# First attention chunk: its steps re-ordered, probabilities and the next keys' split moved behind the last head, scores two heads ahead, one weight load on GpSimd's queue

## The chip, the cores and the metric

One core of a Trainium2 chip runs the whole program. The metric is the time of one execution on the device in microseconds. The kernel is written with a tile framework: the program lists instructions, the framework places buffers, draws the semaphores, and puts the instructions of each engine into one fixed order before anything runs. At run time each engine takes its own list strictly in order.

## What is computed

```python
# attention with decay: B, H, S, D = 2, 8, 576, 64
cum = cumsum(log(clip(f, 1e-4, 1)))
scores = q @ k.T / sqrt(D) + (cum[:, None] - cum[None, :])   # causal
x = softmax(scores) @ v                                       # -> [1152 tokens, 512]
# mixture of 4 experts, p = domain_probs / (sum + 1e-9)
out = sum_e p[:, e:e+1] * (relu(x @ w1[e]) @ w2[e])           # 512 -> 1024 -> 512
# a plain MLP: h = out @ w_in; (h * sigmoid(1.702 h)) @ w_out  # 512 -> 2048 -> 512
```

All of it is float32 to the reference's accuracy. The products are made from a rounded part ("hi") and a remainder ("lo") of each operand, three matmuls for one product.

## The kernel before, in words

The 1152 tokens are cut into four attention chunks: rows 0 to 255 and 256 to 575 of each of the two batches. Chunk 0 (256 rows, 8 heads) is "plain": its queries and keys are float32 with one row more for the decay. It is done first, in twelve steps written out by hand in `first_step(i)`, L830. The experts' first layer then starts on chunk 0 while the other chunks' attention (`attention()`, L872) is interleaved with it by the framework.

One head of chunk 0 goes through these stages:

- `emit_scores` (L660, TensorE): two query tiles against the keys.
- `emit_max` (L690, VectorE): the decay mask is added and the row minimum taken, out of PSUM.
- `emit_exp` (L706, ScalarE), with the row sums.
- `emit_norm` (L713 and L714 on VectorE, L716 on GpSimd): the reciprocal sum, and the scaling of the two tiles.
- `first_tr` (L818, TensorE): three 128x128 transposes into a PSUM bank; `first_copy` (L828) takes them to SBUF.
- `emit_pv` (L772, TensorE): two heads at a time, probabilities times values.
- `emit_x2` (L72 on ScalarE, L783 on VectorE): splits the output of two heads into hi `xh` and lo `xl`.
- `emit_first(k)` (L979, TensorE): the twelve products of the experts' first layer that need heads 2k and 2k+1 alone. The fourth call also takes the result through Relu (L988) and makes its remainder (L989).

Between these stages the steps carry other work. `split_w` (L242, through L72) rounds a 128x512 piece of the expert weights on ScalarE; `split_rest` makes its remainder one step later (L250), on GpSimd for the first four pieces ("a") and on VectorE for all others. `prep_keys` and `prep_queries` split the keys and queries of the next chunk's first pair of heads (L72, L579, L597). `turn(n)` (L1199) issues n bfloat16 matmuls of 512 columns that compute nothing that is used: 11 ahead of the first scores (`WARM`) and `FILL[i]` in step i.

What `first_step` issues is tied in program order on each engine by `in_turn` (L794), that is, TensorE, VectorE, ScalarE and GpSimd take it in the order in which it is written. Instructions written later (the attention of the other chunks) may still be placed among it by the framework. `load_pair` takes two weight pieces (512 KB) at a time through SyncE's queue into one of four buffers `wst`; the queue's own order is written out for the start by `keep_in_program_order` (L80).

`make_probabilities` (L456) normalises the 4 expert weights of each token with six small VectorE instructions on 128x9 or 128x36 elements; its result is first read by L1169.

Of the kernel before, what the change touches and what calls it, by code (L numbers as in the profile page):

```python
# [7 lines left out]
F32 = mybir.dt.float32  # L8
# [10 lines left out]
SA = 256  # L19
# [14 lines left out]
NTILE = NT // 128  # L34
NBLK = 12
NMOE = 8
WARM, FILL = 11, (4, 3, 3, 2, 2, 2, 3, 3,)


class Halves:  # L40
# [11 lines left out]
def attn_moe_mlp(ctx: ExitStack, tc: tile.TileContext, qk0, qk1, qk2, v0, vp, fg, dp, wa_moe, wb_moe, wa_mlp, wb_mlp, out):  # L52
# [6 lines left out]
    nc = tc.nc  # L59
# [16 lines left out]
    def load(out, in_):  # L76

        ins = nc.sync.dma_start(out=out, in_=in_)
        if start[0]:
            tc.keep_in_program_order(ins)  # L80
# [127 lines left out]
    def load_owed():  # L208

        while w_owed[0] and w_loaded[0] < len(w_pairs):  # L210
            kind, v_, g = w_pairs[w_loaded[0]]
            b = visits[v_][0]
            if b < NMOE:
                src = (wa_moe if kind == "a" else wb_moe)[b, g:g + 2]
            else:
                i = m_order.index((kind, v_, g))
                if m_made[0] < i + 2:
                    return
                src = wm[i:i + 2]
            w_owed[0] -= 1  # L220
            w_loaded[0] += 1
            t = wst_p.tile([128, 2, 512], F32, tag="wst", name="wst")
            load(t, src.rearrange("g p c -> p g c"))
            raw_w[kind, v_, g] = t[:, 0, :]
            raw_w[kind, v_, g + 1] = t[:, 1, :]

# [313 lines left out]
    def load_plain_late():  # L540
        for i in (1, 0):
            load(groups[4][i][0:64], qk0[1, 1 - i].rearrange("d (g s) -> d g s", g=4))
        load_plain_values(0)
        load_pair()
        load_pair()
        load_plain_values(4)

    def load_heads(p, h0):
# [79 lines left out]
    def emit_scores(c, u):  # L628


        hs, tiles = u
        out = []
        for q0 in tiles:
            w = min(q0 + 128, S)
            if plain(c):
                st = heads[c, hs[0]]
                mm = [(0, w, [(st["qd"][:, q0:q0 + 128], st["kd"][:, :w])])]
            else:
                p = pass_of[c]
                st = pairs[p, hs[0]]  # L640
                (hi, lo), o = st["qs", c], 2 * (q0 - CH[c][1])
                zs = [(0, w, (0,)), (0, w, (1,))] if q0 < 512 else [(0, 288, (0, 1)), (288, S, (0, 1))]
                mm = [(a, z, [(t[:, o + 128 * g:o + 128 * g + 128], st["ks"][:, g, a:z]) for g in gs for t in (hi, lo)])
                      for a, z, gs in zs]
            pts = []
            both = not plain(c) and w <= 256
            for a, z, _ in mm:
                if plain(c):
                    if q0 == 0:
                        bank = ps_s.tile([128, 512], F32, tag="s", name="s")  # L650
                    pts.append(bank[:, q0:q0 + w])
                else:
                    if not both or not pts:
                        bank = ps_s.tile([128, 512], F32, tag="s", name="s")
                    pts.append(bank[:, 256:256 + w] if both and pts else bank)
                out.append((q0, w, a, z, pts[-1]))
            n = len(mm[0][2])
            for i in range(n):
                for pt, (a, z, lr) in zip(pts, mm):
                    nc.tensor.matmul(pt[:, :z - a], lhsT=lr[i][0], rhs=lr[i][1], start=i == 0 and not (both and pt is not bank),  # L660
                                     stop=i == n - 1, skip_group_check=both)
                    if i == 0 and z == w and not plain(c) and not both and (c not in MASKED or w == S):
                        nc.tensor.matmul(pt[:, q0 - a:w - a], lhsT=identr, rhs=tri2 if w == S else tri, start=False, stop=False)
                if both and i == 0:
                    nc.tensor.matmul(bank.rearrange("p (g k) -> p g k", g=2)[:, :, q0:w], lhsT=identr,
                                     rhs=tri.unsqueeze(1).to_broadcast([128, 2, 128]), start=False, stop=False,
                                     skip_group_check=True)
        raw_s[c, u] = out
# [151 lines left out]
    def first_copy(h):  # L820

        pt = first_t.pop(h)
        ph = pt_p.tile([128, 4, SB], F32, tag="ph", name="ph").rearrange("p i q -> p (i q)")
        ph_of[0, h] = [ph[:, :SA], ph[:, SA:SA + 128]]
        if h == 7:
            round_act(ph[:, :SA + 128], pt[:, :SA + 128])
        else:
            nc.vector.tensor_copy(ph[:, :SA + 128], pt[:, :SA + 128])  # L828

    def first_step(i):  # L830

        n = len(first_seq)
        p, h0 = passes[1], 0
        prep = [(7, lambda: prep_keys(p, h0, 0)), (7, lambda: prep_keys(p, h0, 1)), (9, lambda: prep_keys(p, h0, 2)),
                (9, lambda: prep_queries(p, h0, 1, (0,))), (9, lambda: prep_queries(p, h0, 1, (1,)))]
        for j in (0, 1) if i == 0 else (i + 1,):
            if j < n:
                emit_scores(*first_seq[j])
        if 3 <= i < n + 3:
            emit_pv(0, i - 3)  # L840
        if i >= 7 and x_used[0] < x_made[0] and x_used[0] < 3:
            emit_first(x_used[0])
            x_used[0] += 1
        if i < n:
            emit_max(*first_seq[i])
            emit_exp(*first_seq[i])
# [1 line left out]
            emit_norm(*first_seq[i - 1])  # L848
        if 2 <= i < n + 2:
            first_copy(i - 2)  # L850
        if 3 <= i < n + 3:
            emit_x2(0, i - 3)
        split_rest()
        for kind, p0 in (("a", 2), ("b", 6)):
            if 0 <= i - p0 < 4:
                split_w(kind, 0, i - p0)
                pass
        for j, fn in prep:
            if i == j:
                fn()  # L860
        if i < len(FILL):
            turn(FILL[i])
        if 1 <= i <= n:
            first_tr(i - 1)
        if i == 0:
            load_cum(p, h0)
        if i == 8:
# [4 lines left out]
    def attention():  # L872
# [16 lines left out]
        for i in range(len(seq) + L_X2 + 1):  # L889
            done = None  # L890
            new = [k for k in nxt if first[k] == i + LEAD]
            new_q = [k for k, j in first_q.items() if j == i + LEAD]
            last_pool = [j for j in nc.cur_bb.bb.instructions if j.engine == nc.gpsimd.engine][-1]
            with tc.issue_after(last_pool) if i == 0 else ExitStack():
                for k in new:
                    prep_parts(*k)
                for k in new_q:
                    prep_queries(*k)
            for k in [k for k in nxt if first[k] == i + 2]:
# [65 lines left out]

    first_p = []

    def emit_first(k, last=False):

        v_, b, c = units[0]  # L970
        for g in range(4):
            if k == 0:
                if g % 2 == 0:
                    first_p.append(ps_tile())
# [241 lines left out]
    load_plain(0)  # L1216
    dp_raw = load_probabilities()
    load_plain(4)


    for a, z in ((0, SA), (SA, S)):
# [9 lines left out]
            load_plain_late()  # L1231
    nc.vector.tensor_scalar(out=fr, in0=cum, scalar1=1.0 / NEG, scalar2=None, op0=ALU.mult)
    nc.scalar.dma_start(out=cumd, in_=fr)
    dpn = make_probabilities(dp_raw)
    load_heads(passes[1], 0)
    for _ in range(2):
        load_pair()
# [15 lines left out]
        while ready[0] < c:  # L1253
            pull()

    x_used = [0]
    for i in range(len(first_seq) + 4):
        in_turn(first_step, i)
    ready[0] = 0

    pin_from = [None, 0]
# [115 lines left out]
    late_by = [3]  # L1377
    rest_gen, rest_from = [], seq.index((1,) + units[6])
    cv_due = [0]
    in_turn(emit_first, 3, True)  # L1380
    for i, (kind, v_, b, c) in enumerate(seq):
        if kind == 1 and c < NCH:
            drain(c)
# [161 lines left out]
```

## Time and profile before

| | us |
|---|---|
| median of 3 runs | 687.72 (687.02 to 688.67) |
| the profiled execution, its own time | 687.52 |
| span from its first to its last instruction | 685.8 |
| TensorE busy | 676.4 (99%) |
| VectorE busy | 531.0 (77%) |
| ScalarE busy | 353.6 (52%) |
| GpSimd busy | 244.7 (36%) |

PE is TensorE's matmuls, PEld its weight loads, DVE VectorE, ACT ScalarE, POOL GpSimd, SP SyncE; a "q" behind an engine means its instruction queue. Times in the rows count from the span's start. In a timeline row the first number is the start, the second the time from the start of the first to the end of the last of its instructions, and the brackets hold the idle time of the engine just before them and what ended it. TensorE's matmuls overlap, so that the start of the next row says more about their pace than their own length.

### The profile page before, as it was taken

To read this page: it belongs to the slowest core of one execution; us is meant where nothing else is said; L and a number is where in the kernel's file an instruction comes from. 1 tells how busy PE (TensorE), PEld (TensorE's weight loads), DVE (VectorE), ACT (ScalarE), POOL (GpSimd) and SP (SyncE) were. 2 spreads that over 40 slices of the span, in tenths; PEclk is the share of its full clock that TensorE was granted. 3 is DMA by queue.
4 is the path that set the end of the run, shared out by engine and by line. 5 is a ranking of instruction groups with operands and counts; after the bars stand their busy time and mean duration, and the time that the engine had idled before them with its cause. 6 is when DMAs were issued, how large, how long until landed. Compare 5 with 4: busy or idle time off the path is not lost.

```text
span 685.8 us, 11068 instructions
## 1 busy us (share of the span) xinstructions
PE 676.4 (99%) x3921; PEld 596.8 (87%) x3921; DVE 531.0 (77%) x1097; ACT 353.6 (52%) x821; POOL 244.7 (36%) x302
## 2 busy tenths in 40 slices
PE   8998999999999999999999999999999999999997
PEld 4797889889888898898898898898999998998986
DVE  6896767788698778777987879767799989988532
ACT  5768767667633735635336253362447453552420
POOL 6886577463342454543135324132003300120000
PEclk9999999999999999999999999999999999999999
DMA  8796637145232135053531423413332534441012
GB/s 254 232 307 245 232 114 246 27 151 169 93 123 92 38 117 169 32 159 133 170 108 48 153 77 108 127 41 100 119 108 77 168 124 153 141 153 62 1 46 93
DMA packets 41063, 87.59 MB, mean 128 GB/s; under 512 B 3720, under 2 KB 5776, under 8 KB 40752
## 3 DMA queue, kind: packets, MB, share of 16 engines
q1 hardware_dynamic: 40680, 84.75, 38.0%
q0 software_dynamic: 288, 2.10, 0.8%
q8 instruction: 31, 0.51, 0.3%
q14 instruction: 24, 0.20, 0.1%
q10 hardware_dynamic: 40, 0.04, 0.0%
HBM read 73.98 MB, written 12.88 MB: 127 GB/s over the span
## 4 chain that ended last, share of the span: by engine, by line
PE 90%; DVE 4%; POOL 2%; DMA 1%; ACT 1%; issue 1%; SPq 0%; POOLq 0%; DVEq 0%
PE m L1127 41%; PE m L1002 23%; PE m L958 15%; PE s L660 4%; PE x L772 3%; PE t L734 3%; DMA qr<-in_qk_dram 1%; POOL e L716 1%; PE m L1283 1%; DMA dpraw<-in_dp_dram 1%; POOL qlo L597 1%; POOL qhi L69 1%; DVE acc L1171 0%; POOL ks L579 0%; DVE wf L434 0%
## 5 line engine op out<-in xcount | busy, mean ns | idle before, releaser
L1127 PE MATMUL m<-whi,hh 128*128 128x512 f32 x392 | 109.6, 393 | 0.0
L1127 PE MATMUL m<-wlo,hh 128*128 128x512 f32 x392 | 108.3, 391 | 0.0
L1127 PE MATMUL m<-whi,hl 128*128 128x512 f32 x392 | 108.2, 390 | 0.0
L250 DVE TENSOR_TENSOR wlo<-wst,whi 128x512 fp32r<-128x512 f32 x132 | 101.5, 783 | 6.3 <-ACT whi L72 5.8
L1013 POOL TENSOR_TENSOR hl<-jc,hh 128x320 fp32r<-128x320 f32 (+1 forms) x60 | 53.1, 888 | 141.1 <-ACT hh L72 141.0
L72 ACT ACTIVATE whi<-wst 128x512 fp32r<-128x512 f32 x136 | 80.6, 624 | 26.3 <-PE m L1127 14.2
L1127 PEld LDWEIGHTS m<-wlo,hh 128*128 128x128 f32 x392 | 73.3, 188 | 15.5
L1127 PEld LDWEIGHTS m<-whi,hl 128*128 128x128 f32 x392 | 73.4, 188 | 15.2
L1127 PEld LDWEIGHTS m<-whi,hh 128*128 128x128 f32 x392 | 71.9, 188 | 12.5
L271 POOL TENSOR_TENSOR sr<-wst 128x256 f32<-128x256 f32 x20 | 18.1, 903 | 149.4 <-DMA wst<-wm 79.6
L716 POOL TENSOR_SCALAR e<-e,sm 128x128 f32<-128x128 f32 (+4 forms) x72 | 44.9, 636 | 48.3 <-DVE sm L714 31.7
L1011 ACT ACTIVATE jc<-jc 128x320 f32<-128x320 f32 (+1 forms) x60 | 27.1, 451 | 54.6 <-DVE jc L1008 54.2
L1171 DVE SCALAR_TENSOR_TENSOR acc<-m,dpn,acc 128x512 f32<-128x512 f32 x63 | 46.5, 744 | 7.8 <-PE m L1127 7.6
L958 PE MATMUL m<-xh,whi 128*128 128x256 f32 (+2 forms) x256 | 51.1, 315 | 0.3 <-ACT xh L72 0.3
L958 PE MATMUL m<-xh,wlo 128*128 128x256 f32 (+2 forms) x256 | 50.6, 313 | 0.0
L958 PE MATMUL m<-xl,whi 128*128 128x256 f32 (+2 forms) x256 | 50.5, 314 | 0.0
L706 ACT ACTIVATE e<-e,mx 128x128 f32<-128x128 f32 (+4 forms) x72 | 41.7, 581 | 10.3 <-DVE mx L690 9.9
L958 PEld LDWEIGHTS m<-xh,whi 128*128 128x128 f32 x256 | 41.2, 189 | 2.2 <-ACT xh L72 0.6
L1110 ACT ACTIVATE m<-m 128x384 f32<-128x384 f32 x48 | 23.0, 479 | 37.1 <-DVE m L1008 35.5
L958 PEld LDWEIGHTS m<-xh,wlo 128*128 128x128 f32 x256 | 41.3, 189 | 0.8
L958 PEld LDWEIGHTS m<-xl,whi 128*128 128x128 f32 x256 | 41.0, 189 | 0.6
L1040 ACT ACTIVATE u<-m 128x320 f32<-128x320 f32 (+2 forms) x26 | 11.2, 432 | 50.5 <-PE m L1002 50.5
(174 smaller groups left out, 1510.1 us busy)
## 6 DMA issues: line engine op xcount, KB each, us to landing
wst<-in_wa_moe_dram SPq DMA_DIRECT2D x28, 512.0 KB, 4.2
wst<-in_wb_moe_dram SPq DMA_DIRECT2D x28, 512.0 KB, 4.3
mst<-in_wa_mlp_dram SPq DMA_DIRECT2D x16, 512.0 KB, 3.7
wm<-wf SPq DMA_DIRECT2D x32, 256.0 KB, 4.0
mst<-in_wb_mlp_dram SPq DMA_DIRECT2D x16, 512.0 KB, 4.2
wst<-wm SPq DMA_DIRECT2D x16, 512.0 KB, 3.9
cb<-cumd SPq DMA_DIRECT2D x16, 256.0 KB, 4.4
qr<-in_qk_dram SPq DMA_DIRECT2D x8, 384.0 KB, 4.6
```

The lines of the kernel that those rows point to most:

```text
L72: return nc.scalar.activation(out=out, in_=in_, func=AF.Copy)
L250: (nc.gpsimd if v_ == 0 and kind == 'a' and g < 4 else nc.vector).tensor_sub(lf, raw, f(hf))
L660: nc.tensor.matmul(pt[:, :z - a], lhsT=lr[i][0], rhs=lr[i][1], start=i == 0 and not (both and pt is not bank), stop=i == n - 1, skip_group ...
L706: nc.scalar.activation(out=e[:, off:off + w], in_=e[:, off:off + w], func=AF.Exp, scale=-1.0, bias=mx, accum_out=sm[:, 0, k:k + 1])
L716: nc.gpsimd.tensor_scalar(out=e[:, off:off + w], in0=e[:, off:off + w], scalar1=sm[:, 0, i:i + 1], scalar2=1.0, op0=ALU.mult, op1=ALU.mult)
L958: nc.tensor.matmul(p[:, :n], lhsT=w[:, k, :], rhs=x[c][:, k, :], start=(j == 0 and k == 0), stop=(j == 2 and k == 3))
L1002: nc.tensor.matmul(p[:, :WN], lhsT=w[a][:, k, :], rhs=x[z][:, k, :], start=start and j == 0 and k == 0, stop=stop and j == 2 and k == 1, s ...
L1011: nc.scalar.activation(out=r, in_=r, func=AF.Relu)
L1013: nc.gpsimd.tensor_sub(hl[:, g, :], r, f(hh[:, g, :]))
L1110: nc.scalar.activation(out=p[:, :n], in_=p[:, :n], func=AF.Gelu_apprx_sigmoid)
L1127: nc.tensor.matmul(p, lhsT=h_tile(v_, b, c, j, x, k), rhs=wb[v_, k][w].rearrange("p a c -> p (a c)"), start=i == 0 and k == 0, stop=i == 2 ...
L1171: nc.vector.scalar_tensor_tensor(out=a, in0=p, scalar=d, in1=a, op0=ALU.mult, op1=ALU.add)
```

## The change

The order of the steps of chunk 0 is written anew:

- The six VectorE instructions of `make_probabilities` move from ahead of the first head to step 10.
- Scores are issued two heads ahead instead of one; heads 2 and 5 use a third PSUM bank.
- The transposes of head i-2 stand near the head of step i; before, those of head i-1 stood at the end of it.
- The output split of a pair of heads (`emit_x2`) comes a step after its product for heads 1 and 3; `emit_first` is placed by hand, its second call cut in two halves.
- The first weight pieces are rounded in steps 0 to 3 (before 2 to 5), the next four in steps 7 to 10 (before 6 to 9).
- The transposed probabilities of head 7 are copied by VectorE (before by ScalarE).
- The key split of the next chunk's first pair starts in step 8 (before 7); ScalarE's part for the pair after it may not come before the last ScalarE instruction of the steps.
- `FILL` goes from 22 matmuls to 4.
- The first 512 KB of weights are loaded through GpSimd's queue, ahead of the masks; the second 512 KB stand in SyncE's queue ahead of both loads of values; the third and fourth are issued where they were.

```diff
-WARM, FILL = 11, (4, 3, 3, 2, 2, 2, 3, 3,)
+WARM, FILL = 11, (1, 1, 1, 1, 0, 1)
+X2_AT = {5: 1, 7: 3, 8: 5, 10: 7}
...
+            if w_loaded[0] == 1:
+                tc.keep_in_program_order(nc.gpsimd.dma_start(out=t, in_=src.rearrange("g p c -> p g c")))
+            else:
+                load(t, src.rearrange("g p c -> p g c"))
...
+        load_pair()
         load_plain_values(0)
-        load_pair()
-        load_pair()
         load_plain_values(4)
...
-                        bank = ps_s.tile([128, 512], F32, tag="s", name="s")
+                        bank = ps_tile() if hs[0] % 3 == 2 else ps_s.tile([128, 512], F32, tag="s", name="s")
...
-        if h == 7:
-            round_act(ph[:, :SA + 128], pt[:, :SA + 128])
-        else:
-            nc.vector.tensor_copy(ph[:, :SA + 128], pt[:, :SA + 128])
+        nc.vector.tensor_copy(ph[:, :SA + 128], pt[:, :SA + 128])
...
-        prep = [(7, lambda: prep_keys(p, h0, 0)), (7, lambda: prep_keys(p, h0, 1)), (9, lambda: prep_keys(p, h0, 2)),
+        prep = [(8, lambda: prep_keys(p, h0, 0)), (9, lambda: prep_keys(p, h0, 1)), (9, lambda: prep_keys(p, h0, 2)),
...
-        for j in (0, 1) if i == 0 else (i + 1,):
+        for j in range(3) if i == 0 else (i + 2,):
...
-        if i >= 7 and x_used[0] < x_made[0] and x_used[0] < 3:
-            emit_first(x_used[0])
-            x_used[0] += 1
+        if 2 <= i < n + 2:
+            first_tr(i - 2)
+        for k, gs in {6: [(0, range(4))], 8: [(1, (0, 1))], 9: [(1, (2, 3))], 10: [(2, range(4))]}.get(i, ()):
+            emit_first(k, gs)
...
-        if 3 <= i < n + 3:
-            emit_x2(0, i - 3)
-        split_rest()
-        for kind, p0 in (("a", 2), ("b", 6)):
+        if i in X2_AT:
+            emit_x2(0, X2_AT[i])
+        if i == 10:
+            made_p.append(make_probabilities(dp_raw))
         for j, fn in prep:
             if i == j:
                 fn()
+        split_rest()
+        for kind, p0 in (("a", 0), ("b", 7)):
...
-        if 1 <= i <= n:
-            first_tr(i - 1)
...
+                for j in nc.cur_bb.bb.instructions[begin:]:
+                    if i == 0 and j.engine == nc.scalar.engine:
+                        keep_order([first_act[0], j])
...
     load_plain(4)
+    load_pair()
...
-    dpn = make_probabilities(dp_raw)
```

## Rows read from the trace of the kernel before

**Rows 1.** The page: busy time of each engine, share of the span, instructions.
```profile
PE 676.4 (99%) x3921; PEld 596.8 (87%) x3921; DVE 531.0 (77%) x1097; ACT 353.6 (52%) x821; POOL 244.7 (36%) x302
```
**Rows 2.** Windows: stretch, its length, each engine's busy time, granted clock, DMA share, GB/s.
```profile
8.46:26.40 17.94, 16.87 (x108) 10.86 (x107) 13.23 (x70) 13.57 (x44) 11.86 (x21) 1.00 0.92 312
26.40:47.50 21.10, 20.75 (x143) 18.70 (x141) 20.71 (x40) 14.87 (x32) 18.54 (x17) 1.00 0.86 278
47.50:62.50 15.00, 13.05 (x101) 11.29 (x100) 10.34 (x36) 10.86 (x29) 12.84 (x16) 1.00 0.59 205
```
**Rows 3.** Windows of L1199 alone: TensorE's and its loads' busy time, clock, DMA.
```profile
6.24:21.90 15.66, 5.27 (x19) 1.69 (x19) 1.00 1.03 329
```
**Rows 4.** Timeline of VectorE.
```profile
6.32 0.18 DVE L461 TENSOR_TENSOR dps<-dpraw 128x9 f32<-128x9 f32 x1 [0.74 <-DMA dpraw<-in_dp_dram]
...
8.46 0.28 DVE L690 CUSTOM_DVE_ANT_0 e<-s,raw 128x128 f32<-128x128 f32 x1
...
17.18 0.28 DVE L690 CUSTOM_DVE_ANT_0 e<-s,raw 128x128 f32<-128x128 f32 x1
...
17.73 0.21 DVE L713 TENSOR_SCALAR sm<-sm 128x1 f32<-128x1 f32 x2
...
18.06 0.54 DVE L828 COPY ph<-t 128x384 f32<-128x384 f32 x1
...
21.55 0.42 DVE L783 TENSOR_TENSOR xl<-x,xh 128x256 fp32r<-128x256 f32 x1 [1.33 <-ACT xh L72]
...
26.38 2.54 DVE L250 TENSOR_TENSOR wlo<-wst,whi 128x512 fp32r<-128x512 f32 x2
...
47.00 0.55 DVE L690 CUSTOM_DVE_ANT_0 e<-s,cb 128x384 f32<-128x384 f32 x1
```
**Rows 5.** Timeline of GpSimd.
```profile
1.70 0.94 POOL L524 MEMSET acc<- 1x1024 f32 x1
...
10.34 1.74 POOL L716 TENSOR_SCALAR e<-e,sm 128x128 f32<-128x128 f32 x4 [1.83 <-DVE sm L714]
...
19.11 1.27 POOL L250 TENSOR_TENSOR wlo<-wst,whi 128x512 fp32r<-128x512 f32 x1
...
25.71 0.82 POOL L716 TENSOR_SCALAR e<-e,sm 128x128 f32<-128x128 f32 x2 [1.43 <-PE x L772]
```
**Rows 6.** Timeline of ScalarE.
```profile
26.77 1.39 ACT L72 ACTIVATE ks<-kq 64x576 fp32r<-64x576 f32 x2
28.19 0.49 ACT L72 ACTIVATE ph<-t 128x384 f32<-128x384 f32 x1
...
32.31 0.58 ACT L988 ACTIVATE hh<-m 128x512 fp32r<-128x512 f32 x1
```
**Rows 7.** Timeline of TensorE.
```profile
6.37 1.55 PE L660 MATMUL s<-raw 65*128 65x128 f32 x8
...
27.05 0.49 PE L818 MATMUL t<-identr,e 128*128 128x128 f32 x3
...
47.61 0.50 PE L660 MATMUL s<-ks,qhi 128*128 128x512 f32 x1
...
48.86 0.64 PE L958 MATMUL m<-xh,whi 128*128 128x256 f32 x4
...
52.37 0.40 PE L660 MATMUL s<-ks,qhi 128*128 128x288 f32 x1 [0.54 <-DVE mx L690]
```
**Rows 8.** L380, loads through GpSimd's queue: ns min/median/max, first and last start; landing.
```profile
L380 POOL DMA_DIRECT2D tsl<-tsd x1: 538/538/538, 304.5 to 304.5; - x1
...
DMA to landing us min/median/max: 5.4/6.2/7.1
```
**Rows 9.** The first two weight loads of SyncE's queue, columns as in rows 8.
```profile
L78 SPq DMA_DIRECT2D wst<-in_wa_moe_dram x2: 433/450/468, 6.8 to 7.3; - x2
DMA to landing us min/median/max: 5.2/5.6/6.0
```
**Rows 10.** A window among the first loads, columns as in rows 2.
```profile
5.00:6.00 1.00, 1.00 (x5) 0.25 (x2) 0.55 (x2) 0.00 (x0) 0.95 (x4) 1.00 0.13 16
```

More of the change, by code (lines that the diff above doesn't have):

```diff
@@ L222, in load_owed @@
             t = wst_p.tile([128, 2, 512], F32, tag="wst", name="wst")
-            load(t, src.rearrange("g p c -> p g c"))
+            if w_loaded[0] == 1:
+                tc.keep_in_program_order(nc.gpsimd.dma_start(out=t, in_=src.rearrange("g p c -> p g c")))
+            else:
+                load(t, src.rearrange("g p c -> p g c"))
             raw_w[kind, v_, g] = t[:, 0, :]
@@ L850, in first_step @@
             first_copy(i - 2)
-        if 3 <= i < n + 3:
-            emit_x2(0, i - 3)
-        split_rest()
-        for kind, p0 in (("a", 2), ("b", 6)):
-            if 0 <= i - p0 < 4:
-                split_w(kind, 0, i - p0)
-                pass
+        if i in X2_AT:
+            emit_x2(0, X2_AT[i])
+        if i == 10:
+            made_p.append(make_probabilities(dp_raw))
         for j, fn in prep:
@@ L860, in first_step @@
                 fn()
+        split_rest()
+        for kind, p0 in (("a", 0), ("b", 7)):
+            if 0 <= i - p0 < 4:
+                split_w(kind, 0, i - p0)
         if i < len(FILL):
             turn(FILL[i])
-        if 1 <= i <= n:
-            first_tr(i - 1)
         if i == 0:
@@ L893, in attention @@
             last_pool = [j for j in nc.cur_bb.bb.instructions if j.engine == nc.gpsimd.engine][-1]
+            begin = len(nc.cur_bb.bb.instructions)
             with tc.issue_after(last_pool) if i == 0 else ExitStack():
@@ L966, in attn_moe_mlp, with emit_first @@
     first_p = []
-    def emit_first(k, last=False):
+    def emit_first(k, gs=range(4), last=False):
         v_, b, c = units[0]
-        for g in range(4):
+        for g in gs:
             if k == 0:
@@ L1254, in drain @@
             pull()
-    x_used = [0]
+    made_p = []
     for i in range(len(first_seq) + 4):
         in_turn(first_step, i)
+    first_act = [j for j in nc.cur_bb.bb.instructions if j.engine == nc.scalar.engine][-1:]
+    dpn = made_p[0]
     ready[0] = 0
@@ L1379, in attn_moe_mlp @@
     cv_due = [0]
-    in_turn(emit_first, 3, True)
+    in_turn(emit_first, 3, range(4), True)
     for i, (kind, v_, b, c) in enumerate(seq):
```

## The prediction

> **What bounds the kernel now.** I read the page first: TensorE is busy 99% of the span [rows 1], so time can be won where it does work that nobody needs, or waits for others. Both lie near the start. In the stretch from 6.24 to 21.90 us, 5.27 us of its busy time are the filler matmuls [rows 3]; over all of the first chunk there are 22 of them. So the high busy share there says nothing, and what paces that stretch must be sought in the other engines. Next come the windows [rows 2]. From 8.46 to 26.40 us no engine but TensorE is full: VectorE has 13.23 of 17.94 us, so 4.71 us idle. From 26.40 to 47.50 both are full: VectorE 20.71 of 21.10 us, TensorE 20.75. From 47.50 to 62.50 VectorE has a third of its time free and TensorE lacks 1.95 us. The reader should keep these two pictures apart: a first stretch bound by hand-offs between engines, and a second in which VectorE has no time to give. The change works on the first; what it is worth is decided in the second.
>
> The timelines show the hand-offs. VectorE's first maximum starts at 8.46 us, right behind the probabilities that begin at 6.32 after a wait of 0.74 us for their load [rows 4], while the scores were issued at 6.37 [rows 7]. Later VectorE stands 1.33 us before an output remainder, because it waits for a product of the same step [rows 4]. GpSimd scales the last head at 25.71 us [rows 5]; ScalarE copies that head's transposes only at 28.19, behind 1.39 us of key splitting for a later pair [rows 6]. The Relu that closes the chunk starts at 32.31 [rows 6].
>
> **The change, step by step.**
>
> *Front.* Without the probabilities VectorE waits for scores alone. Eight score matmuls take 1.55 us from 6.37 [rows 7], so a head's four are there at about 7.2; the first maximum moves from 8.46 to 7.2, by 1.26 us.
>
> *Steps 0 to 4.* From the first maximum to the first scaling it was 10.34 - 8.46 = 1.88 us [rows 4, 5]; so the first scaling starts at 7.2 + 1.9 = 9.1. The weight remainders, 1.27 us each, now come in steps 1 to 4, each behind a scaling of 0.82 us [rows 5]. That is 2.09 us a step on GpSimd. VectorE's own step is 0.55 (maximum) + 0.33 (reciprocal sum) + 0.54 (copy) = 1.42 us by the starts and the copy's length [rows 4], so GpSimd is the pace: four steps, 8.4 us, and a fifth scaling ends at 9.1 + 8.4 + 0.8 = 18.3.
>
> *Heads 5 to 7.* Nothing is left on GpSimd but scalings. A loop of copy, maximum, reciprocal sum, scaling, transposes serves two heads, since transposes now belong two steps back: 0.54 + 0.55 + 0.33 + 0.82 + 0.49 [rows 4, 5, 7] and some 0.4 for hand-offs, my estimate, make 3.1 us, or 1.55 a head. From below VectorE allows 1.42; from above, the pace before, counted over all heads: (25.71 - 10.34)/7 = 2.2 [rows 5]. I take 1.55: the last scaling ends at 18.3 + 4.7 = 23.0, where it was 25.71 + 0.82 = 26.53. That is 3.5 us earlier (1.6 to 3.9).
>
> *Tail of the chunk.* From that scaling to the Relu it took 32.31 - 26.53 = 5.8 us. The copy of head 7 no longer stands behind ScalarE's 1.39 us, of which the end of the transposes (27.54) and the copy's start (28.19) show 0.65 as waiting [rows 6, 7]. But it now stands behind a weight remainder on VectorE, 1.27 us each in the pair at 26.38 [rows 4]. I let the two cancel; the ends are 0.65 less and 1.3 more. The Relu then starts at 28.8 instead of 32.31: TensorE has the chunk done **3.5 us earlier** (0.3 to 4.6).
>
> *Filler.* 18 of 22 matmuls go, at 5.27/19 = 0.28 us [rows 3]. They lay in waits, so I cost them at nothing; their cover was the idle time that now shows as such.
>
> *Scores two ahead, third bank.* They take nothing away but order: TensorE meets the next scores before transposes that wait for GpSimd. The gain is in the cadence above. Two more banks are taken from the ring of three, after which both result banks of the first layer find their predecessors (filler, head 2) long read. Nothing.
>
> *First weights by GpSimd's queue.* Such an issue takes 0.54 us of GpSimd for 1 MB, which lands 5.4 to 7.1 us later [rows 8]; here it is half that size, and GpSimd is free for it when its memset ends at 2.64 [rows 5]. So it lands at 8.0 to 9.7 us. ScalarE wants it after the first exponential, about 8.8; late by up to 1 us it costs nothing yet, for GpSimd still has a scaling ahead of the remainder. The second pair stands one issue further ahead than the first did, which left SyncE at 6.8 and landed 5.2 to 6.0 us later [rows 9]: 11.4 to 12.2, wanted in step 2 behind the third exponential, about 11.5. Bound 0 to 0.7. Behind it in SyncE's queue both value loads are later by one issue or earlier by one, with room of some us. I take nothing for all this.
>
> [...] The row first: between 5 and 6 us the DMA engines stood at 0.13 [rows 10], so there is a hole for these 512 KB. [...] I go by the row.
>
> *What the dense stretch takes.* VectorE's work grows: the copy of head 7, 0.54 us, and the probabilities, moved from a place where VectorE had little else to step 10. They took 8.46 - 6.32 = 2.14 us there; six at the 0.18 of the first make 1.1 [rows 4]. I take 1.3, nearer the latter, since all six are of that size. So 1.8 us more in a stretch that is 98% full. VectorE's own account: it starts 1.26 us earlier and had 4.71 idle. In the new order, up to 23.0 us, it works 8 x 1.42, three output remainders at 0.42 and one weight remainder of 1.27, 13.9 us of the 15.8 from 7.2; but each instruction starts some 0.08 us before the one ahead ends (17.73 + 0.21 and the reciprocal, then 18.06), so idle is nearer 3.1 than 1.9, an estimate. The gain on VectorE is 1.26 + 4.71 - 3.1 - 1.8 = **1.1 us** (up to 2.3 with the smaller idle, 0.3 with probabilities at 2.14).
>
> So TensorE could be 3.5 us earlier and VectorE 1.1. Which counts shows at 47 us: VectorE's maximum ends at 47.55 and TensorE's next scores start at 47.61 [rows 4, 7], no slack; at 52.37 it stood 0.54 us for another. What TensorE can do in the meantime is work that needs no maximum: the weight group at 48.86, three rows of four matmuls up to 50.30, is 1.44 us [rows 7], and could be taken ahead. So 1.1 + 1.4 = 2.5 us are kept, between the ends of 1.1 and 3.5. **687.5 - 2.5 = 685.0** for the profiled execution; the median of the runs is 0.2 above it, so 685.2.
>
> **Rivals.**
>
> *VectorE gives no more than its own gain.* If the framework leaves the waiting scores where they are, TensorE waits 2.4 of its 3.5 us from 33 to 53. For it: the 98% and the zero slack at 47.61. Against: the weight remainders in that stretch are ready some us before use, so they could slide. 687.7 - 1.1 = 686.6, within the noise. Chance 0.28.
>
> *All is kept.* If those remainders slide behind the maxima, the full 3.5 us remain: 684.2. For it: VectorE has 4.7 us free from 47.50 to 62.50 [rows 2]. Against: the order is fixed ahead of the run. Chance 0.13.
>
> *The clock falls (slower).* [...] Chance 0.11.
>
> [...]
>
> *A worse order by chance.* The framework draws the rest of the order anew; one more wait like that at 52.37, or three, costs 0.5 to 1.6 us. Chance 0.06, half of it slower.
>
> **How the numbers follow.** My forecast has 0.42, with its own range 684.4 to 686.3. A difference of 0.2%, 1.4 us, is about what a measurement of this kernel can tell from none. Faster by more: the forecast and the full gain, 0.55. Slower by more: the clock and half of the odd orders, 0.14. The rest, 0.31, is the same. The range 683.5 to 688.8 takes in the full gain, VectorE's bound and the small losses, and leaves out the clock and what exceeds the full gain, under 2 in 10.
>
> **What would show it.** Right: a first maximum near 7.2, GpSimd scaling and weight remainder back to back to 18, a last scaling that ends near 23, a Relu near 28.8, clock 1.00. Then look for waits of TensorE for maxima between 33 and 55: some 1 us of them is in the forecast, none would give 684.2, 2.4 us 686.6. Wrong: the first exponential or rounding waits for weights past 10 us; scores start later than 6.4 by more than 0.6; the clock shows under 1.00 between 8 and 20; the last scaling ends after 25.

## Result and the profile after

The changed kernel takes 698.66 us (median of 4 runs, 695.76 to 699.52) against 687.72 for the kernel before. It is 10.9 us slower; 685.2 was predicted. The ratio is 1.0148, 95% interval 1.0132 to 1.0164 (ratios here and below are not quotients of the medians, which would be 1.0159). Its profiled execution took 698.62 us.

The page of the changed kernel, answering to [rows 1], shows next to nothing of this: TensorE's share fell from 99 to 98%.

```profile
PE 683.2 (98%) x3904; PEld 602.1 (86%) x3904; DVE 533.1 (77%) x1098; ACT 353.0 (51%) x820; POOL 243.0 (35%) x303
```

Its 3904 instructions of TensorE are 17 fewer than in [rows 1]: the new `FILL` adds up to 5 matmuls, and the trace has five of them behind the first scores. So 17 of the 22 fillers went. The list of changes, the prediction and the expectations below say 18 gone and 4 left.

Line numbers shift a little between versions: L663, L693, L719, L992 and L1131 of the changed kernel are L660, L690, L716, L988 and L1127 before (L1129 in some versions below). L1131 makes the products of the second layer, the experts' and, late in the program, the MLP's.

Its windows (columns as in [rows 2]; the last three numbers are granted clock, DMA share, GB/s) show it at once. First two of the stretches of [rows 2], then some of 4 us.

```profile
8.46:26.40 17.94, 17.94 (x79) 13.34 (x79) 9.94 (x59) 9.59 (x36) 9.95 (x17) 0.62 0.96 324
26.40:47.50 21.10, 17.45 (x89) 12.93 (x88) 18.80 (x37) 10.74 (x23) 13.21 (x15) 0.84 0.52 172
...
4.00:8.00 4.00, 2.53 (x9) 0.96 (x8) 1.53 (x4) 1.28 (x1) 3.48 (x9) 1.00 1.01 266
8.00:12.00 4.00, 4.00 (x17) 3.20 (x17) 2.63 (x18) 2.84 (x11) 1.84 (x5) 0.65 0.94 259
12.00:16.00 4.00, 4.00 (x14) 3.21 (x13) 1.24 (x8) 1.87 (x9) 2.81 (x4) 0.50 1.03 393
16.00:20.00 4.00, 4.00 (x17) 2.44 (x15) 1.56 (x9) 2.08 (x8) 3.38 (x6) 0.50 1.07 358
...
24.00:28.00 4.00, 3.92 (x31) 2.88 (x28) 3.30 (x20) 2.76 (x10) 1.65 (x4) 1.00 0.62 237
36.00:40.00 4.00, 1.99 (x7) 0.86 (x5) 3.90 (x6) 1.42 (x3) 3.80 (x4) 0.98 1.02 343
40.00:44.00 4.00, 2.43 (x5) 1.67 (x6) 4.00 (x9) 1.29 (x4) 1.43 (x2) 0.50 0.81 272
```

Two things are to be seen. From 12 to 20 us the clock is at 0.50, and TensorE reads as fully busy, but with 14 and 17 matmuls in 4 us (2 and 1 of them filler); in the trace of before, at full clock, the same stretches hold 27 and 24 (5 and 4 of them filler). Here a full busy share means slow matmuls. And from 36 to 44 it is the other way round: 12 matmuls, TensorE idle for 3.6 of 8 us, VectorE full.

The timeline of TensorE in the changed kernel gives the places.

```profile
7.77 1.58 PE L663 MATMUL s<-raw 65*128 65x128 f32 x8 [1.47 <-DMA raw<-raw]
9.16 1.48 PE L663 MATMUL m<-raw 65*128 65x128 f32 x4
...
35.69 0.63 PE L1131 MATMUL m<-whi,hh 128*128 128x512 f32 x2
36.96 0.73 PE L1131 MATMUL m<-whi,hh 128*128 128x512 f32 x2 [0.64 <-ACT hh L992]
37.52 0.62 PE L1131 MATMUL m<-wlo,hh 128*128 128x512 f32 x2
39.08 0.49 PE L1131 MATMUL m<-wlo,hh 128*128 128x512 f32 x1 [0.93 <-DVE wlo L254]
40.48 0.80 PE L1131 MATMUL m<-wlo,hh 128*128 128x512 f32 x1 [0.92 <-DVE wlo L254]
42.36 0.80 PE L663 MATMUL s<-ks,qhi 128*128 128x512 f32 x1 [1.08 <-DVE mx L693]
...
48.37 1.09 PE L1131 MATMUL m<-whi,hl 128*128 128x512 f32 x4
```

The first scores start 1.40 us later than in [rows 7], behind the decay row of the queries and keys (`raw<-raw`, a load of 4 KB). Eight of them take 1.58 us, but the next four take nearly as long (1.48): the clock halves at that point (1.00 from 8.00 to 9.16 us, 0.50 from 9.16 to 10.70). The closing Relu on ScalarE starts at 34.80, 2.49 later than in [rows 6]:

```profile
34.80 0.58 ACT L992 ACTIVATE hh<-m 128x512 fp32r<-128x512 f32 x1
```

In the trace of before TensorE has the first and the last of the groups shown at these places:

```profile
33.40 0.62 PE L1127 MATMUL m<-whi,hh 128*128 128x512 f32 x2
...
39.82 1.09 PE L1127 MATMUL m<-whi,hl 128*128 128x512 f32 x4
```

By the last group (48.37 against 39.82) 8.55 us are lost, 6.1 of them behind the Relu. VectorE in the changed kernel, its first maximum and the same stretch:

```profile
8.82 0.29 DVE L693 CUSTOM_DVE_ANT_0 e<-s,raw 128x128 f32<-128x128 f32 x1 [3.15 <-PE s L663]
...
33.60 0.66 DVE L465 TENSOR_TENSOR dps<-dpraw 128x9 f32<-128x9 f32 x1
34.29 1.09 DVE L467 TENSOR_TENSOR dps<-dps,dpraw 128x9 f32<-128x9 f32 x2
35.42 0.75 DVE L582 TENSOR_TENSOR ks<-kq,ks 64x576 fp32r<-64x576 f32 x1
36.20 0.69 DVE L468 TENSOR_SCALAR dps<-dps 128x9 f32<-128x9 f32 x1
36.92 0.22 DVE L469 RECIPROCAL dps<-dps 128x9 f32<-128x9 f32 x1
37.17 1.25 DVE L470 TENSOR_TENSOR dpn<-dpraw,dps 128x36 f32<-128x36 f32 x1
38.34 3.49 DVE L254 TENSOR_TENSOR wlo<-wst,whi 128x512 fp32r<-128x512 f32 x3
41.76 0.54 DVE L693 CUSTOM_DVE_ANT_0 e<-s,cb 128x384 f32<-128x384 f32 x1
```

The six probability instructions take 3.91 us (1.3 was predicted), three weight remainders 3.49, and only then comes the first maximum of the next chunk, at 41.76. In the trace of before it starts at 31.61:

```profile
31.61 0.56 DVE L690 CUSTOM_DVE_ANT_0 e<-s,cb 128x384 f32<-128x384 f32 x1
```

The rest is lost late. Two rows of TensorE that both traces have, the last attention product and the last group of four with these operands in the second layer, first in before, then in the changed kernel:

```profile
193.90 2.28 PE L772 MATMUL x<-ph,vd 128*64 128x320 f32 x20
679.30 1.07 PE L1127 MATMUL m<-whi,hh 128*128 128x512 f32 x4
...
202.95 2.27 PE L775 MATMUL x<-ph,vd 128*64 128x320 f32 x20
690.29 1.07 PE L1131 MATMUL m<-whi,hh 128*128 128x512 f32 x4
```

The changed kernel is 9.05 us behind at the first of them and 10.99 at the second: 1.94 us more are lost in between.

### The profile page after: what moved, and what is told of

Its sections match the earlier page's. It is cut to its first block, busy times and chain, and to the rows that moved or that the text cites. A ratio compares the mean times of both kernels' runs of the same rounds, so it can differ in the third digit from the quotient of the medians.

```text
span 696.9 us, 11033 instructions
## 1 busy us (share of the span) xinstructions
PE 683.2 (98%) x3904; PEld 602.1 (86%) x3904; DVE 533.1 (77%) x1098; ACT 353.0 (51%) x820; POOL 243.0 (35%) x303
## 4 chain that ended last, share of the span: by engine, by line
PE 90%; DVE 5%; DMA 2%; ACT 2%; issue 1%; DVEq 0%; ACTq 0%; SPq 0%
PE m L1131 39%; PE m L1006 22%; PE m L962 15%; PE s L663 4%; PE x L775 4%; PE t L737 3%; DVE wlo L254 1%; PE m L983 1%; DVE tr L335 1%; DMA mst<-in_wb_mlp_dram 1%; DMA wst<-in_wa_moe_dram 1%; PE t L821 1%; DVE hl L1120 1%; PE m L1289 1%; DMA raw<-raw 0%
## 5 line engine op out<-in xcount | busy, mean ns | idle before, releaser
L1131 PE MATMUL m<-whi,hh 128*128 128x512 f32 x392 | 110.3, 396 | 0.6 <-ACT hh L992 0.6
L1131 PE MATMUL m<-wlo,hh 128*128 128x512 f32 x392 | 109.1, 393 | 1.8 <-DVE wlo L254 1.8
L1131 PE MATMUL m<-whi,hl 128*128 128x512 f32 x392 | 108.5, 391 | 0.0
L1131 PEld LDWEIGHTS m<-wlo,hh 128*128 128x128 f32 x392 | 73.9, 189 | 18.2 <-DVE wlo L254 2.6
L1131 PEld LDWEIGHTS m<-whi,hl 128*128 128x128 f32 x392 | 73.8, 189 | 15.5
L1131 PEld LDWEIGHTS m<-whi,hh 128*128 128x128 f32 x392 | 72.5, 190 | 13.7 <-ACT hh L992 1.1
L719 POOL TENSOR_SCALAR e<-e,sm 128x128 f32<-128x128 f32 (+4 forms) x72 | 44.4, 629 | 49.3 <-DVE sm L717 33.8
```

Of the source, the lines that this page charges most:

```text
L719: nc.gpsimd.tensor_scalar(out=e[:, off:off + w], in0=e[:, off:off + w], scalar1=sm[:, 0, i:i + 1], scalar2=1.0, op0=ALU.mult, op1=ALU.mult)
L1131: nc.tensor.matmul(p, lhsT=h_tile(v_, b, c, j, x, k), rhs=wb[v_, k][w].rearrange("p a c -> p (a c)"), start=i == 0 and k == 0, stop=i == 2 ...
```

## Experiments

Theories at the outset: **A**, the filler kept TensorE's clock up, and without it the clock falls; **B**, the early load delays what the first scores need, and the clock falls behind that wait; **C**, the probabilities behind the last head make VectorE late. Later came **D**, the late remainders of the "b" pieces do that, and **E**, the two additional banks shift the ring of result banks. (In the expectations of g3 and g4 the letters E and F stand for other theories, which are written out there.)

The executions of the changed kernel and of its near relatives, four of each, lie 2 to 8 us apart, so that medians among them that differ by 2 to 3 us have overlapping intervals; where that is so, it is said.

### Filler, first load, more warm-up

```diff
# e1: the changed kernel (e3: before, with the line of the change instead)
-WARM, FILL = 11, (1, 1, 1, 1, 0, 1)
+WARM, FILL = 11, (4, 3, 3, 2, 2, 2, 3, 3,)
# e2: the changed kernel
-WARM, FILL = 11, (1, 1, 1, 1, 0, 1)
+WARM, FILL = 18, (1, 1, 1, 1, 0, 1)
# e4: before
+            if w_loaded[0] == 1:
+                tc.keep_in_program_order(nc.gpsimd.dma_start(...))
...
+        load_pair()
         load_plain_values(0)
-        load_pair()
-        load_pair()
...
     load_plain(4)
+    load_pair()
```

e1: 

> The changed kernel with the filler of the kernel before (22 matmuls instead of 4) in the steps of the first chunk. Theory A, the missing filler let the clock fall: granted clock 1.00 from 8 to 47 us, and the time falls from 698.7 to between 685 and 689 us. Theory B, the 1.47 us in which TensorE waits for the first heads' decay row (6.30 to 7.77 us) let it fall: the wait is still there, the clock is still at half for 13 us or more, 694 to 700 us.

e2: 

> The changed kernel with 18 instead of 11 filler matmuls ahead of the first scores, so that TensorE is busy through the wait from 6.30 to 7.77 us; the steps keep their 4. Theory B: no idle time ahead of the scores, clock 1.00 throughout, 685 to 689 us. Theory A: the clock falls all the same between 9 and 14 us, since the steps after it have as little filler as before; 694 to 700 us.

e3: 

> The kernel before with only the filler of the change (4 matmuls instead of 22). Theory A: the clock falls to half between 8 and 20 us, and the time rises by 4 to 12 us to 692 to 700. Theory B: the first scores still start at 6.4 us, no wait, the clock stays at 1.00, 686 to 689 us.

e4: 

> The kernel before with only the change to the weight loads (first 512 KB by GpSimd's queue, second ahead of the values). Both theories: the first scores start at about 7.8 instead of 6.4 us, because 512 KB more lie ahead of the decay row. Theory A: with all the filler in place the clock stays at 1.00; up to 1.4 us slower than before, 687 to 689 us. Theory B: the clock falls, 692 to 700 us.

| | us | ratio to before, 95% |
|---|---|---|
| e1 | 696.87 | 1.0143 [1.0115, 1.0170] |
| e2 | 695.73 | 1.0121 [1.0106, 1.0136] |
| e3 | 690.62 | 1.0044 [1.0030, 1.0059] |
| e4 | 689.28 | 1.0017 [1.0005, 1.0029] |

Filler taken from the kernel before costs 3.0 us (e3), with half clock in its trace (0.50 from 12 to 16 us), less than the 4 to 12 us of theory A. Given back to the changed one (e1) it moves the median by 1.8 us, which is not clear of noise: there TensorE waits 2.31 us for the decay row, the clock falls all the same (0.56 from 8 to 12 us), as B said, and the Relu starts at 34.92, no earlier than without the filler. The load by itself (e4) makes the first scores late, at 7.49 us, but with the filler of before and a wait of 1.14 us the clock stays at 1.00, and little is lost. e2 is the telling one: with seven more matmuls ahead of the scores its windows show a clock of 1.00 up to 36 us, as B said, though the steps have as little filler as in the changed kernel, and behind a late front the first chunk runs at the pace that was predicted. GpSimd's timeline in e2:

```profile
10.72 0.83 POOL L719 TENSOR_SCALAR e<-e,sm 128x128 f32<-128x128 f32 x2 [2.25 <-ACT whi L73]
...
18.89 0.83 POOL L719 TENSOR_SCALAR e<-e,sm 128x128 f32<-128x128 f32 x2
...
23.39 0.83 POOL L719 TENSOR_SCALAR e<-e,sm 128x128 f32<-128x128 f32 x2 [0.72 <-DVE sm L717]
```

That is 2.04 us a step, then 1.5 a head. ScalarE's Relu in e2 starts 2.24 us ahead of [rows 6]:

```profile
30.07 0.58 ACT L992 ACTIVATE hh<-m 128x512 fp32r<-128x512 f32 x1
```

And yet e2 takes 695.73 us, as A had expected, 8 us more than before. So what A and B describe is some 3 us of the 10.9 by the medians (2.9 from the changed kernel to e2, not clear of noise), and the rest is lost behind the first chunk.

### Where the probabilities stand

```diff
# g1: the changed kernel; g2: also FILL of before; g4: also the load later, "a" a step later
-        if i == 10:
-            made_p.append(make_probabilities(dp_raw))
...
+    dpn = make_probabilities(dp_raw)
# g3: the changed kernel with FILL of before, probabilities behind the whole first chunk
     in_turn(emit_first, 3, range(4), True)
+    made_p.append(make_probabilities(dp_raw))
```

g1: 

> The changed kernel with the probabilities back ahead of the first head; filler as in the change. Theory C, their six instructions (3.9 us beside GpSimd's key split) hold up VectorE between head 7 and the first layer's remainder: TensorE's waits of 3.5 us between 36 and 43 us go to under 1 and the clock does not fall a second time, 690 to 693 us with the first fall still there. Theory D, the weight remainders that now stand last (three in 3.49 us) hold it up: the waits stay over 2 us, 695 us or more.

g2: 

> As the run before, with the filler of the kernel before as well. Theory C: waits as there, one short fall of the clock at 8 to 15 us at most, 687 to 691 us. Theory D: waits over 2 us stay, 694 us or more.

g3: 

> The changed kernel with the filler of before and the probabilities placed after the whole first chunk, outside the written order. Theory C: like the run with them in front, within 1.5 us, since what counts is only that they do not stand ahead of the first layer's remainder. Theory E, any work added to VectorE's full stretch costs its length: 2 to 4 us slower than with them in front.

g4: 

> Probabilities in front, filler of before, and GpSimd's weight load issued behind the first masks (about 5 us instead of 2.6), the first four pieces rounded one step later. Theory F, that load lies ahead of the first heads' decay row and makes the scores late by 1.4 to 2.3 us: the first scores start at 6.4 us again, the clock stays at 1.00, and the time is 1.5 to 4 us below the run without this edit. If the load costs the front nothing: within 1 us of it.

| | us | ratio to before, 95% |
|---|---|---|
| g1 | 695.73 | 1.0144 [1.0092, 1.0196] |
| g2 | 694.98 | 1.0121 [1.0095, 1.0147] |
| g3 | 697.09 | 1.0141 [1.0119, 1.0163] |
| g4 | 695.77 | 1.0116 [1.0100, 1.0131] |

C as the only cause falls: with the probabilities back in front (g1), and the filler too (g2, which meets D's expectation), and the late load as well (g4), 8 us are still missing. In g4 the first scores start at 6.52 us again, so the load was what held them up (7.77), but the time does not fall below g2's. g3 is 2.1 us slower than g2, within what four runs of each tell; its scores start at 7.96 and its clock falls (0.988 over the profiled span), so it settles nothing on the place of the probabilities. The timeline of TensorE in g4 shows what it waits for now:

```profile
31.88 0.62 PE L1129 MATMUL m<-whi,hh 128*128 128x512 f32 x2
35.73 0.79 PE L663 MATMUL s<-ks,qhi 128*128 128x512 f32 x1 [3.23 <-DVE mx L693]
...
36.96 1.91 PE L1129 MATMUL m<-whi,hh 128*128 128x512 f32 x4
38.67 1.91 PE L1129 MATMUL m<-wlo,hh 128*128 128x512 f32 x4
```

The first chunk ends earlier than before (31.88 against 33.40 in the trace of before); then one wait of 3.23 us for a maximum, and behind it the half clock: four matmuls to the next group take 1.71 us, where they take 0.99 in i2 below. On VectorE in g4, four weight remainders (1.21, 2.58 for two, 1.78 us) stand ahead of that maximum, while earlier, at 21.5 to 24.6, it waited for transposes with nothing to do (0.98 and 0.78 us).

### The remainders earlier, the ring, the order

```diff
# h1: g4; i1: the changed kernel
-        for kind, p0 in (..., ("b", 7)):
+        for kind, p0 in (..., ("b", 5)):
# h2: before, with scores two ahead, third bank, transposes of head i-2; ring counted as before
+                        ps_n[0] -= hs[0] % 3 == 2
# h3: before; h4: the changed kernel, with -= 2
     ready[0] = 0
+    ps_n[0] += 2
```

h1: 

> The late-load version (695.77) with the four b pieces rounded in steps 5 to 8 instead of 7 to 10, so that VectorE makes their remainders from step 6 on, in time it has idle there. Theory (VectorE's remainders, put behind the last head, hold back the first maxima of the next chunk): TensorE's wait of 3.23 us for the first maximum falls under 1 us, the maximum starts 2 to 4 us earlier than 35.1, time 692.5 to 694. Rival (the wait comes from the keys and queries, which VectorE can split only behind head 7, or from a clock that falls again): the wait stays above 2.5 us, time 695 to 696.5.

h2: 

> Before, with the scores two heads ahead, the third bank and the transposes of head i-2 in step i, the ring of result banks counted as before; filler, weight pieces, probabilities, copy of head 7 and loads as before. Theory (the new order of TensorE's instructions is not what costs): clock 1.00 to 33 us, the last scaling earlier than 26.5 by 0.5 to 2 us, time 686.5 to 688. Rival (scores two ahead themselves put transposes and products later and TensorE waits): first L1131 group later than 33.4, time above 689.

h3: 

> Before, with the counter of the ring of result banks moved on by two once the first chunk is issued, which is what the two score banks of heads 2 and 5 do to it in the changed kernel; nothing else. Theory (the some 2 us that the changed kernel loses between 210 and 600 us come from other banks being taken there): nothing changes ahead of 210 us, then 1.5 to 2.5 us are lost, time 689.2 to 690.2. Rival (they come from the later arrival at that stage, or from the order of the remainders): no change, 687.5 to 688.2.

h4: 

> The changed kernel with that counter set back by two once the first chunk is issued; nothing else. By the theory on the ring: 696.2 to 697.2, and the loss in front of 92 us stays at some 9 us. By the rival: 698.2 to 699.

| | us | ratio to before, 95% |
|---|---|---|
| h1 | 690.21 | 1.0035 [1.0020, 1.0050] |
| h2 | 689.81 | 1.0031 [1.0022, 1.0041] |
| h3 | 689.61 | 1.0023 [1.0013, 1.0033] |
| h4 | 696.51 | 1.0120 [1.0089, 1.0151] |

D holds: two steps earlier for four instructions each on ScalarE and VectorE, and 5.6 us are back (g4 to h1), more than the 1.8 to 3.3 expected. The wait of 3.23 us is gone from h1's list.

E holds, too, as far as the counter goes. Moved by two, it costs 2.0 us in the kernel before (h3); in the changed one, moved back, it moves the median by 2.2 (h4), as expected but not clear of noise there. The traces tell it better. TensorE in h3:

```profile
194.15 2.28 PE L772 MATMUL x<-ph,vd 128*64 128x320 f32 x20
681.33 1.07 PE L1127 MATMUL m<-whi,hh 128*128 128x512 f32 x4
```

Between these two rows lie 487.18 us, in before 485.40: 1.78 more. Every version here with the shifted counter takes 1.7 to 2.1 us more than before on this stretch, and none with the counter of before does. In h3 TensorE waits 0.7 and 0.5 us between 205 and 600 us (for L1002's operands from VectorE and ScalarE); before has no such wait there. Whether the bank itself makes them is not shown: with the counter the framework's order changes too (in h3 six groups of four of L1127 stand in a row ahead of L1002's product of `xh` and `sh` at 225.29, in before two, at 223.99).

h2 met its rival: two heads ahead, in the otherwise old order, ends the last scaling 1.0 us earlier (25.52), but the Relu later (32.97), the first second-layer group starts at 35.04 against 33.40, and the time is 689.81. So the new order of TensorE's work is no gain by itself.

### The two causes apart

```diff
# i2: h1 with the ring's counter set back by two
# i4: i2 with the probabilities in step 10, as in the changed kernel
# i3: i2, and
+            elif w_loaded[0] == 9:
+                nc.gpsimd.dma_start(out=t, in_=...)
```

i1: 

> The changed kernel with the four b pieces rounded in steps 5 to 8 instead of 7 to 10; all else as changed. Theory (the late pieces are the largest part of the loss, as they were with the filler in place: 695.8 to 690.2): 4 to 6 us come back, 692.5 to 694.5, TensorE's waits for the second layer's remainders (1.8 us) go. Rival (with the clock at half in the first chunk TensorE is late anyway, so earlier pieces are hidden): above 696.5.

i2: 

> The version with earlier pieces (690.21; filler of before, late load, probabilities in front) with the counter of the result banks set back by two. By the ring's price in the two runs before (2.0 and 2.1): 688.0 to 688.4. Rival (the ring costs only when other things are late): 689.5 or more.

i3: 

> The version with pieces and ring back, and the ninth weight load issued by GpSimd instead of SyncE, where it stood behind decay loads that waited for their buffer until 46.4 us, so that TensorE waited 1.85 us for its rounding at 53 us. Theory (the lead of 1.5 us of the first chunk is lost to that load): no such wait, 686.3 to 687. Rival (another wait takes its place, VectorE or the order): no change, 688 to 688.5.

i4: 

> The version with pieces and ring back, and the probabilities in step 10 as in the changed kernel. Theory (they cost 2 to 4 us of VectorE beside the maxima, of which the first chunk's earlier start gives 1.3 back): 1 to 2.5 us slower than that version, 689.2 to 690.7. Rival (VectorE has room once the pieces are earlier): the same or faster, 687 to 688.3.

| | us | ratio to before, 95% |
|---|---|---|
| i1 | 696.20 | 1.0104 [1.0071, 1.0137] |
| i2 | 687.02 | 0.9994 [0.9985, 1.0004] |
| i3 | 688.85 | 1.0021 [1.0006, 1.0037] |
| i4 | 692.46 | 1.0070 [1.0049, 1.0091] |

i2 is level with before, so the parts that it takes back are enough to explain the loss. It is no exact undoing: the "b" pieces stand in steps 5 to 8, where before had 6 to 9 and the change 7 to 10, the "a" pieces one step earlier than before, and the next keys' split, which the change put a step later, stays there; what that split costs was not tested by itself. i1 alone, the pieces earlier in the changed kernel, lies between its two expectations. i4 differs from i2 only in where six small instructions stand, and is 5.4 us slower, more than the 1 to 2.5 expected. The timeline of TensorE in i2:

```profile
32.00 0.63 PE L1129 MATMUL m<-whi,hh 128*128 128x512 f32 x2
32.75 0.50 PE L663 MATMUL s<-ks,qhi 128*128 128x512 f32 x1
...
33.44 1.15 PE L1129 MATMUL m<-whi,hh 128*128 128x512 f32 x4
34.43 1.07 PE L1129 MATMUL m<-wlo,hh 128*128 128x512 f32 x4
```

The timeline of VectorE in i4, where in i2 the first maximum starts at 32.14:

```profile
29.53 0.65 DVE L465 TENSOR_TENSOR dps<-dpraw 128x9 f32<-128x9 f32 x1
30.22 0.18 DVE L467 TENSOR_TENSOR dps<-dps,dpraw 128x9 f32<-128x9 f32 x1
...
31.93 0.69 DVE L467 TENSOR_TENSOR dps<-dps,dpraw 128x9 f32<-128x9 f32 x1
32.65 0.17 DVE L468 TENSOR_SCALAR dps<-dps 128x9 f32<-128x9 f32 x1
32.85 0.22 DVE L469 RECIPROCAL dps<-dps 128x9 f32<-128x9 f32 x1
33.10 1.03 DVE L470 TENSOR_TENSOR dpn<-dpraw,dps 128x36 f32<-128x36 f32 x1
...
34.66 0.55 DVE L693 CUSTOM_DVE_ANT_0 e<-s,cb 128x384 f32<-128x384 f32 x1
```

And that of TensorE in i4:

```profile
31.61 0.62 PE L1131 MATMUL m<-whi,hh 128*128 128x512 f32 x2
35.27 0.79 PE L663 MATMUL s<-ks,qhi 128*128 128x512 f32 x1 [3.03 <-DVE mx L693]
...
36.49 1.91 PE L1131 MATMUL m<-whi,hh 128*128 128x512 f32 x4
```

i4 even leaves the first chunk 0.39 us earlier (31.61 against 32.00). TensorE then has two matmuls to do and waits 3.03 us. The next score is 2.5 us later than in i2 (35.27 against 32.75), and the half clock behind the wait adds 2.6 by the next score of 512 columns (42.72 against 37.61). (The profiled execution of i4 is its slowest and that of i2 its fastest, so the traces lie further apart than the medians.) So late probabilities (i4) and late pieces (g4) each do the same, and either one is enough. This fits what undoing one of them in the changed kernel gave back: by the medians 2.9 us (g1) and 2.5 (i1), neither clear of noise, against 5.4 to 5.6 once it was the last.

i3 asked where i2's lead goes: its first second-layer group is 1.4 us ahead of before, its end only 0.6 (by the medians). TensorE in i2 waits 1.16 us at 52.36 for a rounding by ScalarE, which waits 1.40 for weights; their load left SyncE only at 47.52, behind decay loads at 46.34. With that load on GpSimd's queue (i3) the wait is gone, but the framework orders the rest anew and the time is 1.8 us longer, above both expectations. So the place of the loss is shown; that it can be won is not.

### What is left: filler and first load

```diff
# j1: i2
-WARM, FILL = 11, (4, 3, 3, 2, 2, 2, 3, 3,)
+WARM, FILL = 11, (1, 1, 1, 1, 0, 1)
# j2: the changed kernel with b in step 5, probabilities in front, ps_n[0] -= 2
```

j1: 

> The version with pieces and ring back (687.02; clock 1.00 throughout) with the filler of the change, 4 matmuls instead of 22. Theory (filler keeps TensorE's clock up and is worth its time): the clock is at half for 5 us or more between 8 and 20, the first chunk ends 2 to 4 us later, 689.5 to 692. Rival (filler lies in waits and is worth nothing, as predicted): 686.5 to 687.5.

j2: 

> The changed kernel with three things back: b pieces in steps 5 to 8, probabilities in front, the ring's counter; the filler of the change and the first load on GpSimd's queue stay. Theory (what is left is the clock of the first chunk and scores that start 1.4 us late): 690 to 693, no wait of TensorE over 1 us for a maximum between 30 and 50. Rival (each of the remaining parts puts the first maxima late again): 694.5 or more.

j1 takes 688.68 us (1.0015 [1.0001, 1.0028]), j2 689.41 (1.0034 [1.0007, 1.0061]). Both medians hide a spread. j1 lies between its two expectations, j2 just below the range of its theory, without a wait of over 1 us for a maximum, as that said. The ten executions of j2, with the granted clock over the span of each:

```
us     686.74  686.82  686.92  687.80  688.23  690.59  691.40  692.08  692.11  695.32
clock   1.000   1.000   1.000   1.000   0.994   0.993   0.993   0.990   0.988   0.985
```

One program, one chip: where the clock held, it is as fast as i2; where it did not, it loses up to 8.6 us. i2, with 22 filler matmuls and the late load, stays between 0.998 and 1.000 in ten executions (686.7 to 688.62). So the 17 filler matmuls less and the early load cost nothing in the executions whose clock held; without that filler, and with that load, it no longer holds in every one.

## Why the prediction was wrong

**Steps 0 to 4, Heads 5 to 7, Tail: right.** e2 has the clock that the prediction assumed. There a step takes 2.04 us (2.09 said), a head 1.5 (1.55), and from the last scaling's end at 24.22 to the Relu it is 5.85 (5.8). In the tail some of this is luck: the copy starts 1.19 us behind the scaling's end, where it was 1.66 before, and what follows it takes 4.66 instead of 4.12. The Relu comes 2.24 us earlier, not 3.5; the missing 1.3 is the front's, whose first scaling starts at 10.72 instead of 9.1.

**Front: wrong.** "The first maximum moves from 8.46 to 7.2"; it came at 8.82. The load on GpSimd's queue, costed as "I take nothing", held up the decay row: the DMA share from 4 to 8 us is 1.01 where the hole of [rows 10] was, and the scores start 1.40 us later. I had watched the keys and not the smallest load behind them. With the load issued later (g4) the scores start at 6.52. The transfer alone, 512 KB at the 329 GB/s of [rows 3], would be 1.6 us, an estimate; the trace shows the 1.40.

**Filler: wrong.** "I cost them at nothing; their cover was the idle time." Taken out of the kernel before, it costs 3.0 us (e3). The rival "the clock falls", at a chance of 0.11, had what came, and "under 1.00 between 8 and 20" the place; no row of before shows a lower clock or what it costs. The real matmuls that every step keeps did not hold the clock up: from 12 to 20 us, at 0.50, they are 12 of 14 and 16 of 17 matmuls in 4 us. In the changed kernel its own share can't be told apart from the front's: less filler lets the clock fall with the scores on time (e3), the late front does so with all the filler back (e1), and with seven more matmuls over the wait ahead of the scores the clock holds without the steps' filler (e2). There the fallen clock, whichever of the two made it fall, costs 4.7 us at the Relu (34.80 against e2's 30.07), of which 2.4 are left at the last attention product (202.95 against 200.58) and 2.9 in the medians (698.66 against 695.73, not clear of noise).

The clock fell behind waits of 1.47 us at the start (the changed kernel) and 3.03 and 3.23 us later (i4, 0.50 from 36 to 40 us; g4, by the 1.71 us for four matmuls), while waits of 1.16 (i2) and 1.85 us (h1) did not lower it (1.00 in the windows around both), so that the length of a wait alone doesn't decide. The column of the granted clock doesn't tell it alone either: in g1 it reads 1.00 from 8 to 16 us, where TensorE does 14 matmuls in each 4 us, as few as the changed kernel at 0.50 (12 to 16 us).

**What the dense stretch takes: the step that failed most.** It forecast a gain of 1.1 us on VectorE and that TensorE could fill 1.4 us with other work. Three things were wrong in it. The probabilities were priced at 1.3 us, though its own rows had 2.14 for them at the old place; beside GpSimd's splits they take 2.9 in i4 and 3.9 in the changed kernel. The sum of work and idle time over 18 us hid where the work stands: the "b" remainders a step later, behind the last head, lie ahead of the first maxima of the next chunk, and idle time at 22 us can't pay for that. And TensorE had two to eight matmuls to do instead, not 1.4 us of work freely placed, because its order is fixed: in g4 the four matmuls at 36.96, whose roundings on ScalarE had ended by 33.32, stand behind the score that waits until 35.73. What the runs show in its place: each of the two delays makes TensorE wait 3 us for the first maximum, with half clock behind the wait, and costs 5.4 us (i4 against i2) and 5.6 us (g4 against h1) instead of giving 2.5. How much both cost at once is shown only roughly: j2, with both and the counter taken back, is 9.25 us faster than the changed kernel, 7.3 without the counter's 1.9, so less than the two together.

**Scores two ahead, third bank: "Nothing" was wrong.** The banks taken for heads 2 and 5 move the ring's counter by two for the rest of the program. That costs 1.7 to 2.1 us behind the last attention product in every trace that has it (2.0 by the medians of h3 and before, 3.2 from h1 to i2, where h1's slightly lower clock counts too). The prediction looked at the nearest users of the ring only.

**The sum.** By the traces the changed kernel is 9.05 us behind before at the last attention product, and e2, whose clock held in the first chunk, 6.68. So some 2.4 us go with the clock of the first chunk, some 6.7 with what came behind it, and 1.9 with the counter; together 11.0. Taking back pieces, probabilities and counter returns 9.25 us of the 10.9 in the median (j2), which leaves 1.7 for the rest, filler and first load among it. Both are single versions with a spread of some us, so this is a rough account. Of the other rivals, "VectorE gives no more than its own gain" looked at the right engine and the right stretch, but bounded the loss by the gain.

## What to carry to other kernels

Before work is moved behind a stage, list what an in-order engine must finish ahead of the first result that TensorE needs next; idle time that an average shows earlier doesn't pay for it, and two delays that hide behind each other must be taken out together before either shows its worth. Filler ahead of and between short matmuls is to be judged by the granted clock and the count of matmuls over many executions, not by whether its time lies in waits. After every edit of the front, compare the late stages too: a shared counter can carry it there.

## What the runs showed of the hardware

- VectorE beside GpSimd, in i4: a 128x512 remainder takes 0.68 us at 25.47, where GpSimd stands still for most of it, 1.20 at 28.07, beside its splits of queries and keys (25.98 to 36.65), and 0.68 again at 34.05, beside them too. Of the small instructions on 128x9 among them, one takes 0.65 and another 0.18. VectorE's copy out of PSUM takes 0.55 at 26.07, beside a split, and 0.56 at 24.66, beside a scaling. So some of VectorE's instructions take longer beside the splits and others do not; what decides it is not shown. The prediction took 0.18 from the row at 6.32 us in [rows 4].
- TensorE can read as 100% busy for 8 us at half clock (the changed kernel, 12 to 20 us, at 0.50); the count of matmuls in a window tells it (14 and 17 in 4 us, 27 and 24 before), the share does not.
- The same program kept a granted clock of 1.000 in four of ten executions and had 0.994 to 0.985 in six (j2).
